# A second cosine table, fewer zero matmuls and a reordered opening in a fused Fourier filter and max-out kernel

## The chip, the cores and the metric

The kernel runs as one program on one core of a Trainium2 chip. The core has a matrix engine (TensorE, "PE" in the profile; its weight loads are listed apart as "PEld"), VectorE ("DVE"), ScalarE ("ACT"), GpSimd ("POOL") and SyncE ("SP"). Each engine works through its own instructions in the order in which the program gives them, and waits where an operand or a buffer is not ready. TensorE writes into PSUM; VectorE and ScalarE copy from there into SBUF. The metric is the device time of the program in microseconds (us). Several executions were timed, and one of them was recorded by the hardware profiler.

## The reference: what is computed

The input x has 8 batches of 3072 tokens with 256 features. Each batch is filtered along its token axis in the frequency domain, and the result goes through a max-out layer of width 1024:

```python
X = np.fft.rfft(x, axis=1)
F = (filt_r + 1j * filt_i)[None, :, :]
y = np.fft.irfft(X * F, n=x.shape[1], axis=1)     # 8 x 3072 x 256

h1 = y @ w1                                       # 24576 x 1024
h2 = y @ w2
out = np.maximum(h1, h2) @ w_out                  # 24576 x 256, float32
```

## The kernel before, in words

The Fourier transform of length 3072 is split as 128 times 24. The kernel uses max(h1, h2) = h2 + max(h1 - h2, 0): the weights `Wd` hold w1 - w2, the ReLU of `y @ Wd` is multiplied by `Wo`, and the part of h2 is one product with `M` = w2 @ w_out, which is made once. Matrix products are in bf16.

**Stages of one batch.** S1 multiplies the tokens with a table of cosines and sines of length 128 (`C1`, 128x128). S2 multiplies with the twiddle table `U`, in 8 groups of frequencies. VectorE (or GpSimd) multiplies the result with the filter table `F` (the "products", tiles `pq`). S3 goes back with the tables `VP` and `VQ`. S4 multiplies with `G1`, the transpose of `C1`, and gives `yt`. After it come `moe_h` (product with `Wd`, ReLU) and `moe_o` (products with `Wo` and `M`, then the output DMA).

**Two forms.** Batches 1 to 7 take the form of the long steady part: `f1` is S1, its result is transposed by way of DRAM (`ad`, `bt`), and `gen_f2` is S2, products and S3. They are interleaved with `moe_h` and `moe_o` of the batch ahead: a loop of 49 x 8 steps calls `moe_h` and `moe_o`, and a dictionary `todo` says at which step a piece of the next batch's work is issued. Batch 0 has nothing to hide behind, so it takes a form of its own, the opening, in which TensorE transposes and nothing goes through DRAM:

- `first_s1(c)`, c = 0 to 5 (lines 428 to 436): S1 for one loaded chunk of x. Eight matmuls of 128x128x128 whose moving operand is `C1` read as `"p (t b a) -> p b a t"`, that is with a step of four elements; then ScalarE copies 128x1024 into `At`.
- `expand_f(g, ri, E)` (lines 113 to 126): sixteen small matmuls with a selection matrix that bring two rows of the real (ri = 0) or imaginary (ri = 1) filter into the order of `F`; engine `E` copies 128x1024.
- `tables_u`, `sines_u` (lines 205 to 273): some forty VectorE instructions and then ScalarE sines make `U`. `tables_pe` (line 280) transposes `U` into `VP`; `tables_q` (line 294) makes `VQ`.
- `first_t1(g, E)` (lines 438 to 447): eight transposes of `At`, copied into `bt[0]` by `E`.
- `first_s2(g, pool)` (lines 455 to 472): S2 of group g, and the two products. With `pool`, ScalarE first copies half of the PSUM tile to `xs` and GpSimd makes the second product.
- `first_s3(g, pq)` (lines 474 to 488): S3 of group g, 32 matmuls, copied by ScalarE into `Zt`.
- `prep_w(k, E)` (lines 323 to 338): k = 0 and 1 transpose w2 into `w2T`; k = 2 and 3 multiply `w2T` by `Wo` into the two halves of one PSUM tile, and k = 3 copies it to `M`.
- `first_t2(j, E)` (line 490): transposes of `Zt` into `zr[0]`, which `s4` reads.
- `spin(pd, n)` (lines 307 to 309): n matmuls of 128x128x512 whose operands are zeros. Their results are overwritten. There are 14 at the start, one at the head of every `expand_f` and every `first_s1`, and two at the head of every `first_s3`.

**What sets the order.** The program text gives each engine its order; nothing reorders it. PSUM has two buffers under each of two tags, `pa` and `pb` (`bank2`, line 88). Up to the group loop the calls take `pa` and `pb` in turn; in the group loop (lines 601 to 621) `first_s2` takes `pb` and all others take `pa`. A call waits until the last but one user of its tag has been copied out. The group loop goes over n = 0 to 7 with group g = order[n], order = (1, 2, 3, 0, 4, 5, 6, 7), and `first_s3` runs two groups behind `first_s2`. The opening ends where `s4(0)` and the first `moe_h` begin (lines 626 to 637).

The loads are issued by GpSimd: the real filter, six chunks of x of batch 0, the imaginary filter, w1 and w2, the chunks of batch 1, and later `Wo`.

## Time and profile before

| | us |
|---|---|
| median of 8 runs (lowest 546.56, highest 549.3) | 546.82 |
| the profiled execution | 546.95 |
| its span in the trace | 545.0 |
| outside the span in that execution (546.95 - 545.0) | 1.95 |
| TensorE busy | 520.3 (95%) |
| ScalarE busy | 337.3 (62%) |
| VectorE busy | 322.8 (59%) |
| GpSimd busy | 72.7 (13%) |
| first matmul on the filter (after it has landed) | 8.62 |
| first matmul of `s4(0)` | 56.48 |

The times of a timeline are in us from the start of the span. A line gives the start, the length, the engine, the source line, the operation with output<-input and shapes, the count, and in brackets how long the engine sat idle before it and what ended that. A matmul's length includes its way through the array, so the next one starts before it ends. A busy share in a table by stretches is in us of the stretch.

### The profile page before, as it was taken

The numbers are of one execution on the slowest core, as the hardware profiler recorded it, in microseconds if no ns is written. First come the engines' busy times: TensorE is split into PE (matmuls) and PEld (weight loads), VectorE is DVE, ScalarE is ACT, GpSimd is POOL, SyncE is SP. The second block draws the span as 40 slices with busy tenths as digits, with TensorE's granted clock in tenths as the row PEclk, the third lists the DMA queues.
The fourth block names the chain that finished last, engine by engine and source line by source line (L and its number), as shares of the span: only waits on it lengthen the run. The fifth ranks groups of instructions, "written<-read, shape, count | busy, mean of one in ns | idle before, by whom it ended". The sixth has DMA issues, their size and how long they took to land.

```text
span 545.0 us, 12576 instructions
## 1 busy us (share of the span) xinstructions
PE 520.3 (95%) x5389; PEld 352.0 (65%) x5389; DVE 322.8 (59%) x427; ACT 337.3 (62%) x590; POOL 72.7 (13%) x126
## 2 busy tenths in 40 slices
PE   7988899999999999999999899999999999999992
PEld 3655566667666666676667666666667666677771
DVE  8576759524872476438763677448863788344331
ACT  6866647775787578845775467755775565554540
POOL 6184011011001110021001100021000000000000
PEclk9999999999999999999999999999999999999997
DMA  8972297779477965599378955599377925611111
GB/s 161 285 117 41 112 169 156 174 232 242 110 214 222 213 164 161 161 215 218 110 218 201 201 146 163 163 229 212 108 211 191 168 81 144 163 40 78 79 40 77
DMA packets 67596, 87.07 MB, mean 160 GB/s; under 512 B 3986, under 2 KB 48276, under 8 KB 66452
## 3 DMA queue, kind: packets, MB, share of 16 engines
q1 hardware_dynamic: 51908, 44.31, 35.9%
q0 software_dynamic: 15632, 41.95, 29.3%
q8 instruction: 42, 0.69, 0.6%
q14 instruction: 14, 0.11, 0.1%
HBM read 53.74 MB, written 47.19 MB: 185 GB/s over the span
## 4 chain that ended last, share of the span: by engine, by line
issue 66%; POOL 6%; PE 4%; POOLq 0%
POOL out_dram L552 4%; POOL xb L101 2%; PE po L546 1%; PE ph L521 1%; PE po L541 0%; PE px L408 0%; PE py L505 0%; POOLq L730 0%; POOLq L552 0%; PE pz L389 0%; POOLq L101 0%
## 5 line engine op out<-in xcount | busy, mean ns | idle before, releaser
L526 ACT ACTIVATE gt<-ph 128x512 bf16<-128x512 f32 x307 | 181.9, 599 | 111.3 <-PE ph L521 110.3
L546 PE MATMUL po<-Wo,gt 128*128 128x256 bf16 x1536 | 229.8, 273 | 0.0
L546 PEld LDWEIGHTS <-gt 128*128 128x128 bf16 x1536 | 150.3, 98 | 57.5
L413 DVE TENSOR_TENSOR pq<-px,F 120x1024 bf16<-120x1024 f32 x112 | 131.7, 1218 | 25.3 <-PE px L408 24.4
L548 DVE COPY ot<-po 128x512 f32<-128x512 f32 x96 | 66.3, 690 | 109.4 <-PE po L546 108.8
L393 ACT ACTIVATE zt<-pz 112x512 bf16<-112x512 f32 x112 | 60.8, 594 | 45.4 <-PE pz L389 40.4
L521 PEld LDWEIGHTS <-Wd 128*128 128x128 bf16 x768 | 69.9, 98 | 25.4 <-issue 11.3
L552 POOL DMA_DIRECT2D out_dram<-ot x48 | 25.8, 538 | 445.1 <-DVE ot L548 415.4
L524 DVE TENSOR_SCALAR gt<-ph 128x512 bf16<-128x512 f32 x77 | 52.9, 687 | 35.2 <-PE ph L521 31.3
L453 ACT ACTIVATE at<-pa 128x512 bf16<-128x512 f32 x77 | 46.2, 601 | 11.5 <-PE pa L354 9.2
L354 PE MATMUL pa<-xb,C 128*128 128x512 bf16 x84 | 31.5, 381 | 0.8 <-DVE zr L451 0.8
L505 PE MATMUL py<-G,zr 128*128 128x128 bf16 x384 | 29.7, 219 | 0.7 <-DVE pq L413 0.7
L389 PE MATMUL pz<-pq,VP 56*64 56x256 bf16 x448 | 28.8, 271 | 1.6 <-DVE pq L413 1.6
L505 PEld LDWEIGHTS <-zr 128*128 128x128 bf16 x384 | 24.9, 98 | 6.0 <-issue 3.4
L389 PE MATMUL pz<-pq,VQ 56*64 56x256 bf16 x448 | 28.1, 268 | 0.0
L101 POOL DMA_DIRECT2D xb<-in_x_dram x48 | 26.0, 547 | 7.6 <-PE pa L433 4.1
L408 PE MATMUL px<-bt,U 48*64 48x256 bf16 x448 | 23.9, 281 | 1.8 <-DMA bt<-ad 1.8
L469 DVE TENSOR_TENSOR pq<-px,F 120x1024 bf16<-120x1024 f32 x13 | 15.3, 1219 | 4.5 <-ACT xs L464 2.0
L408 PEld LDWEIGHTS <-U 48*64 48x64 bf16 x448 | 8.5, 104 | 14.1 <-issue 11.8
L389 PEld LDWEIGHTS <-VP 56*64 56x64 bf16 x448 | 13.4, 106 | 3.7 <-DVE pq L413 2.2
L453 ACT ACTIVATE F<-pf 128x1024 bf16<-128x1024 f32 x12 | 12.1, 1022 | 5.6 <-PE pf L125 5.5
L389 PEld LDWEIGHTS <-VQ 56*64 56x64 bf16 x448 | 13.4, 107 | 0.0
(360 smaller groups left out, 588.3 us busy)
## 6 DMA issues: line engine op xcount, KB each, us to landing
out_dram<-ot POOLq DMA_DIRECT2D x48, 512.0 KB, 4.3
xb<-in_x_dram POOLq DMA_DIRECT2D x48, 256.0 KB, 7.6
ad<-at SPq DMA_DIRECT2D x42, 256.0 KB
bt<-ad SPq DMA_DIRECT2D x28, 384.0 KB
zd<-zt SPq DMA_DIRECT2D x56, 192.0 KB
zr<-zd SPq DMA_DIRECT2D x14, 768.0 KB
wf<-in_moe_w_dram POOLq DMA_DIRECT2D x2, 1024.0 KB, 15.1
Fs<-in_filt_r_dram POOLq DMA_DIRECT2D x1, 768.0 KB, 6.9
```

The source lines that it names most:

```text
L101: G.dma_start(out=t_, in_=src[:, 4 * c:4 * c + 4, :])
L389: TE.matmul(pz[c][64 * k:64 * k + 64, i], W[64 * c:64 * c + 56, 2 * g + i, k], pq[k][64 * c:64 * c + 56, ri, i], start=(ri == 0), stop=(ri ...
L393: S.activation(zt[0:ROWS, c, o:o + 2], pz[c][0:ROWS], AF.Copy)
L413: V.tensor_tensor(pq[k][0:FROWS], px[k][0:FROWS].rearrange("p (o i) d -> p o i d", o=1).to_broadcast([FROWS, 2, 2, D]), F[0:FROWS, :, k, 2 ...
L453: S.activation(out_, in_, AF.Copy)
L505: TE.matmul(py[:, n], zr[b][:, 4 * i + n, 128 * dc:128 * dc + 128], G1, start=True, stop=True)
L521: TE.matmul(ph, Wd[:, dc, 128 * j:128 * j + 128], y_[:, dc].rearrange("p a b -> p (a b)"), start=(dc == 0), stop=(dc == 1))
L524: V.tensor_scalar(gt[tt][:, j], ph, 0.0, None, OP.max)
L526: S.activation(gt[tt][:, j], ph, AF.Relu)
L546: TE.matmul(p_, g_[:, jj, 128 * n:128 * n + 128], Wo[:, jj], start=False, stop=(jj == 7))
L548: V.tensor_copy(ot[tt][:, n - 1:n + 1], po[tt])
L552: G.dma_start(out=dst[:, 4 * i:4 * i + 4], in_=ot[tt])
```

## The change: what it does

- A second cosine table `Ct` is made by one VectorE copy at the end of `table_c`; it holds the values of `C1` in the order in which `first_s1` reads them, so that the moving operand is read without a step.
- `expand_f` and `first_s1` lose their one zero matmul each, and `first_s3` keeps one of two. The zero operand shrinks from 128x512 to 128x128; the zero matmuls read it four times over and still have 512 columns.
- Before the group loop `first_t1(3)` comes ahead of `expand_f(1, 1)` and `first_t1(0)` ahead of `expand_f(2, 1)`. In the loop `first_t1(order[n + 4])` moves from the end of an iteration to its head, ahead of `first_s2` and the products.
- `expand_f(7, 0)` moves from n = 1 to n = 3.
- `prep_w(0)` and `prep_w(1)` move from n = 6 and 7 to n = 4 and 5, ahead of `table_g` in n = 4. `prep_w(2)` and `prep_w(3)` move from behind the loop into n = 6, and the copy to `M` goes from VectorE to ScalarE.
- One piece of S1 of batch 1 more (`f1(1, 1)`) is done before `first_t2(0)`, and the rest move up by one.

```diff
     def expand_f(g, ri, E):
         pf = bank2([128, 2, 2, D], FP32, "pf")
-        spin(pf[:, 0].rearrange("p u d -> p (u d)"), 1)
...
-    Sp = init.tile([128, 512], BF16)
+    Sp = init.tile([128, 128], BF16)
...
+    Ct = init.tile([128, 128], BF16)
+
     def table_c():
...
+        V.tensor_copy(Ct.rearrange("p (b a t) -> p t b a", b=2, a=2), C1.rearrange("p (t b a) -> p t b a", b=2, a=2))
...
     def spin(pd, n):
         for _ in range(n):
-            TE.matmul(pd, Sp[:, 0:128], Sp, start=True, stop=True)
+            TE.matmul(pd, Sp, Sp.rearrange("p (o x) -> p o x", o=1).to_broadcast([128, 4, 128]), start=True, stop=True)
...
     def first_s1(c):
         pa = bank2([128, 2, 2, 2, 4, T], FP32, "pa")
-        spin(pa[:, 0].rearrange("p b a n t -> p (b a n t)"), 1)
         for dh in range(2):
             for n in range(4):
                 TE.matmul(pa[:, dh, :, :, n], xb[0, c][:, n, 128 * dh:128 * dh + 128],
-                          C1.rearrange("p (t b a) -> p b a t", b=2, a=2), start=True, stop=True)
+                          Ct.rearrange("p (b a t) -> p b a t", b=2, a=2), start=True, stop=True)
...
     def first_s3(g, pq):
         pz = bank2([128, 2, 512], FP32, "pz")
-        spin(pz[:, 0], 2)
+        spin(pz[:, 0], 1)
...
     first_t1(2, V)
     tables_q(1, S)
+    first_t1(3, V)
     expand_f(1, 1, S)
-    first_t1(3, V)
+    first_t1(0, V)
     expand_f(2, 1, S)
-    first_t1(0, V)
     pend = []
     ring = ["pa"]
     for n, g in enumerate(order):
+        if n < 4:
+            first_t1(order[n + 4], V)
         pend.append(first_s2(g, n in (0, 2, 4)))
-        if n == 1:
-            expand_f(6, 0, S)
+        if n in (1, 3):
+            expand_f(6 + n // 2, 0, S)
         if n < 6:
             expand_f(order[n + 2], 1, S)
         if n == 0:
             load_wo()
         if n == 1:
             fix_f()
-            expand_f(7, 0, S)
         if n in (1, 3, 5):
             prep_wd(n // 2, *wf)
-        if n < 4:
-            first_t1(order[n + 4], V)
+        if n > 1:
+            first_s3(*pend.pop(0))
+        if n in (4, 5):
+            prep_w(n - 4, S)
         if n == 4:
             table_g()
-        if n > 1:
-            first_s3(*pend.pop(0))
-        if n > 5:
-            prep_w(n - 6, S)
+        if n == 6:
+            prep_w(2, S)
+            prep_w(3, S)
     first_s3(*pend.pop(0))
-    prep_w(2, V)
     first_s3(*pend.pop(0))
-    prep_w(3, V)
     zr[0] = zrpool.tile([128, N2, D], BF16, tag="zr", name="zr")
     f1(1, 0, V)
+    f1(1, 1, V)
     first_t2(0, V)
...
-    f1(1, 1, S)
+    f1(1, 2, S)
     s4(0)
-    f1(1, 2, V)
+    f1(1, 3, V)
...
-    for c in range(3, 12):
-        plan(int(0.6 * (c - 2)), f1, 1, c, (S, V)[c % 2])
+    for c in range(4, 12):
+        plan(int(0.6 * (c - 3)), f1, 1, c, (S, V)[c % 2])
```

## The prediction, made before the result was known

> **What bounds the kernel now.** I read the page first, then busy time by stretches, then the timelines of the opening engine by engine, then the waits of the steady part. By stretches (PE, PEld, DVE, ACT, POOL busy us, granted clock, DMA share, GB/s):

> ```profile
> 8.60:22.40 13.80, 13.10 (x221) 8.81 (x220) 9.94 (x17) 10.37 (x13) 4.66 (x8) 1.00 1.09 256
> 22.40:26.80 4.40, 4.39 (x68) 3.12 (x68) 1.98 (x3) 3.30 (x4) 0.00 (x0) 1.00 1.07 309
> 26.80:52.40 25.60, 22.80 (x499) 12.98 (x497) 18.40 (x18) 17.83 (x22) 17.42 (x13) 1.00 0.55 87
> 52.40:56.50 4.10, 2.84 (x52) 2.11 (x52) 1.98 (x3) 0.81 (x1) 0.00 (x0) 1.00 0.00 0
> ...
> 100.00:515.00 415.00, 410.94 (x3943) 281.09 (x3941) 243.25 (x295) 265.11 (x482) 38.65 (x73) 1.00 0.68 169
> ```

> The steady part is TensorE's, at 99%, so a start that is earlier by some time should end the program earlier by as much. The change lies in the four stretches above it. The first two are TensorE's as well, but part of that is zero matmuls. One round of the S1 stretch in TensorE's timeline:

> ```profile
> 12.06 0.39 PE L309 MATMUL pa<-Sp 128*128 128x512 bf16 x1
> 12.29 1.09 PE L433 MATMUL pa<-C,xb 128*128 128x128 bf16 x8
> 13.20 0.40 PE L309 MATMUL pf<-Sp 128*128 128x512 bf16 x1
> ```

> The starts give the spacing: zero matmul 0.23, S1 0.91, zero matmul 0.33, expansion (line 125, 13.53) 0.55, round 2.02 with the next zero matmul at 14.08. So 0.56 of each 2.02 us is zeros. In the group loop (iteration n = 4) it is a chain through ScalarE:

> ```profile
> 39.87 0.41 PE L460 MATMUL px<-bt,U 48*64 48x256 bf16 x8
> 40.21 0.39 PE L309 MATMUL pf<-Sp 128*128 128x512 bf16 x1
> 40.53 0.62 PE L125 MATMUL pf<-Fs,Sel 96*32 96x256 bf16 x16
> ...
> 42.28 0.59 PE L309 MATMUL pz<-Sp 128*128 128x512 bf16 x2 [0.96 <-ACT F L453]
> ...
> 43.30 0.41 PE L460 MATMUL px<-bt,U 48*64 48x256 bf16 x8
> ```

> The reader is to see that S3's bank is the one that ScalarE is emptying: S2 0.34, zeros 0.32, expansion until it lands 0.62, copy 1.02 (line 453, from 41.20) with 0.1 of handing over, two zeros 0.53, S3 0.50, together 3.43, and the iteration took 43.30 - 39.87 = 3.43. All three zero matmuls lie on that chain.

> **The method.** I write down each engine's order after the change and go through it with spacings from the rows: S2 0.34, expansion 0.55, transposes of `At` 0.55 (8 of them), S3 0.50, a zero matmul 0.32, `w2T` transposes 0.56, a half of M 0.78; ScalarE copies 1.02 (0.81 for `Zt`, 0.60 for `xs`), VectorE 1.22 for a filter, 1.15 to 1.22 for a product, 0.69 for `bt`, `at`, `zr`; 0.05 from an end to the one who waits. Done with the order of before, this comes 0.2 to 0.4 us late against the trace: 22.60 for 22.40 at the first transposes of `At`, 27.07 for 26.83 at the first S2, 52.82 for 52.44 at the last S3.

> **First stretch, 8.62 to the first transposes of `At` (22.40).** Eleven zero matmuls go (five at expansions, six at S1), 0.23 to 0.33 each. S1 itself reads `Ct`: its eight matmuls take 0.91 now, and the same shape with an unstepped operand (line 505) starts its successor after 0.44 (56.48 to 56.92). The price lies between 0.44 and 0.91 (its output pattern, which stays, may be what is slow); I take 0.50, nearest to the row of the same shape. TensorE's round would be about 1.1, so TensorE stops being the limit. Next is VectorE, through the copy that makes `Ct`:

> ```profile
> 2.53 0.29 DVE L198 TENSOR_TENSOR uc<-uc,rc 128x128 f32<-128x128 f32 x1
> 2.74 0.15 DVE L211 TENSOR_SCALAR col<-pid 128x1 f32<-128x1 f32 x1
> ...
> 2.86 1.00 ACT L202 ACTIVATE C<-uc,zero 128x32 bf16<-128x32 f32 x4 [0.84 <-DVE uc L198]
> ```

> The copy stands between the first two lines and has to wait for the sines to end at 3.86. Its own length is between 0.11 (memset of 128x64) and 0.96 (line 287, twelve times as large); I take 0.25, by the 0.23 of a 128x128 pass (line 197). The some forty instructions of `tables_u` queue behind it: they start at 4.15 instead of 2.74, 1.4 late, so VectorE's first filter copy starts at 14.3 instead of 12.97 (the first line-451 row there), and the sines of `U` wait until 13.8. From there: filter copies end 15.5, 16.7, 17.9, 19.2. The fifth expansion needs the bank that the first of these frees: 15.55 (TensorE then has idled 1.8 us). S1 of chunk 3 at 16.1, expansion 16.8, S1 of chunk 4 at 17.3; `VP`'s transposes wait for the last sines, 18.5; S1 of chunk 5 at 19.1 (its x landed at 6.25 + 10.9 = 17.15, so no DMA ends this); `At` 19.8 to 20.8; the transposes at 20.9 instead of 22.40. **Gain 1.5.** Without the 1.4 on VectorE it would be 1.1 more; were the copy 0.96 long, 0.7 less.

> [...] Line 433 spaces its matmuls 0.114, line 505 0.055. [...]

> **Second stretch, to the first S2 (26.83).** Before: four transposes, one `VQ` product, two expansions, two zeros: 2.20 + 0.53 + 1.10 + 0.64 = 4.47, measured 4.43. After: the zeros go, `first_t1(4)` moves in: 2.75 + 0.53 + 1.10 = 4.38. **Gain 0.05.** The `bt` copies on VectorE (0.69 in each 0.55 to 1.1) keep pace.

> **Third stretch, S2 of n = 0 to the last S3 (25.61).** Iteration lengths before, from the starts of line 460 (26.83, 28.69, 32.81, 36.42, 39.87, 43.30, 45.56, 47.50) and the last S3 (52.44): 1.9, 4.1, 3.6, 3.4, 3.4, 2.3, 1.9, 4.9. After, by the walk: 1.5, 2.9, 2.9, 3.0, 3.3, 3.3, 2.8, 2.9, in sum 22.65. n = 1 loses one of three expansions (to n = 3) and three zeros. In n = 2 S3 now waits for VectorE, which copies the hoisted `bt` behind two products (to 31.15). In n = 3 it waits for the copy of filter 7, which came in. n = 4 to 6 take `w2T` and M in, each piece waiting for the 1.02 of a filter copy or of the `w2T` copy ahead; the M copy on ScalarE (0.60) frees the bank for S3 of group 6. In the tail S3 of group 7 waits for the last products: S2 45.0, products 45.5 and 46.65 to 47.87, S3 at 47.9. GpSimd is no limit: `w2b` is ready at 34.0 (used at 38.0), `Wd` at 42.9; `Wo` lands by 37 (used at 43.5); SP has nothing in this part. **Gain 2.95.**

> **Fourth stretch, last S3 to `s4(0)` (4.04).** Before, M's copy stood between:

> ```profile
> 54.03 0.69 DVE L451 CAST M<-pm 128x512 bf16<-128x512 f32 x1 [3.33 <-PE pm L335]
> ...
> 54.78 0.71 PE L494 MATMUL pt<-I,Zt 128*128 128x128 bf16 x8 [0.48 <-DVE M L451]
> ...
> 55.52 0.69 DVE L451 COPY zr<-pt 128x1024 bf16<-128x1024 bf16 x1 [0.20 <-PE pt L494]
> ```

> After: S3 lands 0.65, `Zt` 0.81, the added `f1` 0.27, transposes 0.77, `zr` 0.74, `f1(1, 2)` 0.21, in sum 3.45 to 3.5. **Gain 0.55.** The added `f1`'s VectorE copy (0.69) fits while TensorE transposes.

> **Steady part.** One `f1` fewer in it (0.22 a matmul of 512): **gain 0.2.** `f1_read` stays at step 5 with `f1` done a step earlier, and TensorE's waits for a transfer after 57 us are small: line 408 for `bt`, 1.8 us in two waits.

> **Sum.** 1.5 + 0.05 + 2.95 + 0.55 + 0.2 = 5.25; against its own lateness the walk is worth up to 0.4 more. I take 5.5: 546.95 - 5.5 = 541.4 for the profiled execution, which lies 0.13 above the median. Own range of this case 540.0 to 542.8 (`Ct`'s copy, S1 between 0.44 and 0.91, the lateness).

> **Rivals.**

> *TensorE's clock falls (slower).* The first 14 zero matmuls start 0.43 apart until 5.46 and then about half that: TensorE begins at half rate and reaches the full one only after 4.2 us of steady work. Without the zeros it is thinly fed: by the walk 0.5 us of matmuls in the 3.05 before 15.55, then 55 to 75% of most stretches. If the rate falls, each us of the opening at half rate costs about 0.33 by the walk (blocks 1.9 times as long, partly within waits). From 17 us of it on (5.5 / 0.33) there is no gain; half rate throughout the group loop (24 us) gives 549, from 12.3 us on 554. Against it: TensorE stood still from 6.8 to 8.62, and the next expansions were spaced 0.55 as later; from 53.95 to 57.88 it had 1.4 us of work in 3.9, and the next `moe_h` pair took 0.59 as always. The granted clock of 1.00 from 0 to 5 us doesn't show that half rate, so it settles nothing. [...]

> *Half of it: some falls.* Three to ten us at half rate: 1 to 3.3 lost, 542.4 to 544.7.

> [...]

> *The opening is shorter and the end isn't.* Transfers would have to set the pace of the steady part; then 545 to 546.9. Against: DMA share 0.68 there and 1.8 us of waits.

> **How the numbers follow.** The forecast 0.58; clock falls for part 0.16; VectorE 0.08; end not earlier 0.05 (0.03 of it within 0.2% of 546.8, which is what the measurement can tell from none); clock low for 17 us or more 0.13. Faster 0.84, same 0.03, slower 0.13. The range leaves out the slow clock (0.13) and a little below: 539.8 to 546.0.

> **What would show it.** Right: lines 309 of the S1 rounds gone; a VectorE wait for `C` of about 1 us before `Ct`, its first filter copy near 14.3; `At` transposes near 20.9, first S2 near 25.3, last S3 near 47.9, `s4(0)` near 51. Wrong: expansions spaced 1.0 instead of 0.55 anywhere after 8.62, S1 of eight near 0.9, or `s4(0)` near 51 with a span above 541.

## The result and the profile after

The changed kernel takes 543.17 us in the median of its 11 runs (540.34 to 545.37), the kernel before 547.38 in 32 runs (546.27 to 550.82). The ratio is 0.9908, with a 95% interval of 0.9889 to 0.9927: about 0.9% faster. The profiled execution took 541.22 us with a span of 539.1, against 546.95 and 545.0.

The forecast was 541.4 for the profiled execution, in a range of 539.8 to 546.0. Direction and range hold, and the profiled execution is 0.2 below the forecast. The median of the runs is 1.8 above it: between the medians the gain is 4.2 us where 5.5 was forecast. The runs spread over 5 us, and where the median of the kernel before lies 1.1 above its fastest run, that of the changed kernel lies 2.8 above. This is the part that needed explaining.

First the stretches of the prediction in the changed kernel, cut at the same events (columns as before: length, busy us of PE, PEld, DVE, ACT, POOL, granted clock, DMA share, GB/s):

```profile
8.60:20.84 12.24, 9.46 (x210) 6.54 (x210) 10.99 (x20) 9.98 (x12) 4.13 (x7) 0.86 1.09 231
20.84:25.31 4.47, 4.47 (x75) 3.64 (x74) 2.67 (x4) 3.60 (x4) 0.53 (x1) 1.00 1.03 384
25.31:47.79 22.48, 19.10 (x487) 12.78 (x485) 17.75 (x17) 18.14 (x23) 17.35 (x13) 1.00 0.69 115
47.79:51.24 3.45, 1.99 (x40) 1.36 (x41) 1.98 (x3) 0.85 (x2) 0.00 (x0) 1.00 0.00 0
```

The four lengths were 13.8, 4.4, 25.6 and 4.0 before. TensorE's busy time in the first stretch fell from 13.10 to 9.46, and its granted clock from 1.00 to 0.86. The timeline shows the second table's copy on VectorE, and what came late for it (start, length, engine, line, operation):

```profile
2.45 0.29 DVE L199 TENSOR_TENSOR uc<-uc,rc 128x128 f32<-128x128 f32 x1
2.78 1.00 ACT L203 ACTIVATE C<-uc,zero 128x32 bf16<-128x32 f32 x4 [0.76 <-DVE uc L199]
...
3.81 0.56 DVE L206 COPY Ct<-C 128x128 bf16<-128x128 bf16 x1 [1.06 <-ACT C L203]
...
4.04 0.33 DVE L214 TENSOR_SCALAR col<-pid 128x1 f32<-128x1 f32 x1
...
14.33 4.61 DVE L453 CAST F<-pf 128x1024 bf16<-128x1024 f32 x4
```

VectorE waits 1.06 us for `C1`. The row of the copy is 0.56 long, but the next one starts 0.23 after it, against 0.25 in the prediction. VectorE's first filter copy starts at 14.33 where it was 12.97. TensorE's rounds in the same stretch:

```profile
8.86 1.65 PE L124 MATMUL pf<-Fs,Sel 96*32 96x256 bf16 x32 [2.32 <-DMA Fs<-in_filt_r_dram]
10.44 1.03 PE L435 MATMUL pa<-Ct,xb 128*128 128x128 bf16 x8
11.41 1.04 PE L124 MATMUL pf<-Fs,Sel 96*32 96x256 bf16 x16
12.38 0.70 PE L435 MATMUL pa<-Ct,xb 128*128 128x128 bf16 x8
13.01 0.62 PE L124 MATMUL pf<-Fs,Sel 96*32 96x256 bf16 x16
...
15.60 0.62 PE L124 MATMUL pf<-Fs,Sel 96*32 96x256 bf16 x16 [1.41 <-DVE F L453]
```

The expansion at 11.41 takes 1.04, the one at 13.01 takes 0.62: behind the pause from 6.5 to 8.86 the granted clock went to 0.50, from 9.17 to 12.58, and then back to 1.00. Little or nothing of this can have reached the end: until 15.60 TensorE waited 1.41 us for VectorE's first filter copy to end, which the prediction had at 15.55.

In the group loop TensorE waits where the prediction has it wait, in n = 2 for the hoisted `bt` and in n = 3 for the copy of filter 7:

```profile
31.14 0.38 PE L312 MATMUL pz<-Sp 128*128 128x512 bf16 x1 [0.45 <-DVE bt L453]
...
34.70 0.38 PE L312 MATMUL pz<-Sp 128*128 128x512 bf16 x1 [0.62 <-ACT F L455]
```

The end of the opening (from two views, TensorE's and VectorE's timeline):

```profile
49.27 0.38 PE L357 MATMUL pa<-xb,C 128*128 128x512 bf16 x1 [0.58 <-ACT Zt L490]
49.48 0.71 PE L496 MATMUL pt<-I,Zt 128*128 128x128 bf16 x8
...
50.29 0.68 DVE L453 COPY zr<-pt 128x1024 bf16<-128x1024 bf16 x1
...
51.02 0.38 PE L357 MATMUL pa<-xb,C 128*128 128x512 bf16 x1 [0.83 <-DVE zr L453]
51.24 0.61 PE L507 MATMUL py<-G,zr 128*128 128x128 bf16 x8
```

VectorE's copy of M is gone from this chain, and `s4(0)` starts at 51.24 instead of 56.48.

### The profile page after: what moved, and what is told of

It is laid out like the page before. It is cut to its first block, busy times and chain, and to the rows that moved or that the text cites. A ratio compares the mean times of both kernels' runs of the same rounds, so it can differ in the third digit from the quotient of the medians.

```text
span 539.1 us, 12518 instructions
## 1 busy us (share of the span) xinstructions
PE 511.7 (95%) x5359; PEld 349.1 (65%) x5359; DVE 322.2 (60%) x427; ACT 337.6 (63%) x591; POOL 72.6 (13%) x126
## 4 chain that ended last, share of the span: by engine, by line
issue 48%; PE 24%; POOL 4%; DVE 0%; POOLq 0%
PE ph L523 9%; PE po L548 9%; POOL out_dram L554 3%; PE po L543 2%; PE pz L392 1%; POOL xb L101 1%; PE px L411 1%; PE pa L357 1%; PE py L507 1%; DVE pq L416 0%; POOLq L733 0%; POOLq L554 0%; POOLq L101 0%
## 5 line engine op out<-in xcount | busy, mean ns | idle before, releaser
L523 PEld LDWEIGHTS <-Wd 128*128 128x128 bf16 x768 | 69.9, 98 | 25.3 <-issue 11.1
L124 PE MATMUL pf<-Fs,Sel 96*32 96x256 bf16 x256 | 10.6, 296 | 4.6 <-DMA Fs<-in_filt_r_dram 2.3
```

The source lines that it names most:

```text
L523: TE.matmul(ph, Wd[:, dc, 128 * j:128 * j + 128], y_[:, dc].rearrange("p a b -> p (a b)"), start=(dc == 0), stop=(dc == 1))
```

## Experiments

Two theories were to be told apart at first. Theory Z: the zero matmuls on TensorE's way were the cost, and cutting them is the gain. Theory O: the new order, the second table and the move of w2.wo (w2 @ w_out, made by `prep_w`) made it. Theory C stood beside them: a thinly fed TensorE loses its clock, and that makes the spread.

A measure that the falls of the clock before 25 us don't touch is the length from the first S2 to `s4(0)`, called the loop below: 29.65 us before (26.83 to 56.48), 25.93 after (25.31 to 51.24). Unless it is said otherwise, its granted clock was 1.00 in the profiled execution.

### e1: the zero matmuls cut, nothing else

```diff
 before.py, expand_f and first_s1:
-        spin(..., 1)
 first_s3:
-        spin(pz[:, 0], 2)
+        spin(pz[:, 0], 1)
```

> The kernel before with one edit alone: the zero matmuls of expand_f and first_s1 go and first_s3 keeps one. Theory Z (the zeros on TensorE's way were the cost): the walk through the queues gives s4(0) at 51.3 against 56.5, nearly the whole gain: time 0.990 to 0.992 of before. Theory O (the new order, the second table and w2.wo made the gain): at most the zeros that no wait hid, s4(0) at 54 or later, ratio 0.995 to 1.0. Theory C (TensorE's clock falls when it is thinly fed): the granted clock of the runs lies between 0.984 and 0.991 instead of 0.994 and the runs with the lower clock are 1 to 2 us longer each 0.003.

Measured: ratio 0.991 (0.9879 to 0.9942), so the whole gain of the change within the intervals. The loop takes 26.17, 3.48 of the 3.72 that the change takes off. `s4(0)` came at 52.75 and not at 51.3, because the clock fell twice, from 10.94 to 14.35 and from 21.18 to 24.59. The second fall lies in the dense stretch between the first transposes and the first S2, which took 5.43 where it takes 4.4. The stretches of e1:

```profile
7.50:10.94 3.44, 2.16 (x44) 1.66 (x47) 3.23 (x11) 1.73 (x2) 1.44 (x2) 1.00 1.12 216
10.94:14.35 3.41, 3.41 (x45) 2.20 (x46) 3.31 (x7) 2.55 (x4) 1.09 (x2) 0.50 1.13 207
14.35:21.18 6.83, 6.01 (x128) 4.13 (x126) 4.43 (x4) 5.79 (x9) 1.59 (x4) 1.00 1.05 258
21.18:24.59 3.41, 3.41 (x34) 2.29 (x34) 1.38 (x2) 1.46 (x2) 0.53 (x1) 0.50 1.04 405
```

The granted clock (the last column but two) goes straight to 0.50 and back, in pieces of 3.41 us. Over the runs, clocks of 0.990 to 0.991 go with 541.1 to 542.1 us, clocks of 0.980 to 0.986 with 543.2 to 544.5. Theory Z holds, and C in so far as the clocks came out near what it said (0.980 to 0.991); O falls as the main cause.

### e2: the zero matmuls put back into the changed kernel

```diff
 after.py, expand_f and first_s1:
+        spin(..., 1)
 first_s3:
-        spin(pz[:, 0], 1)
+        spin(pz[:, 0], 2)
```

> The changed kernel with all zero matmuls of before put back (30 more), everything else as changed. Theory Z: s4(0) at about 54.2 by the walk, so about half of the gain or less is left: ratio to before 0.994 to 0.997. Theory O: s4(0) stays near 51.5, ratio 0.990 to 0.992. Theory C: the granted clock is back at 0.994 in every run and the runs lie within 1 us of each other, apart from those outliers that before has too.

Measured: ratio 0.9965 (0.9941 to 0.9988); `s4(0)` at 54.39, the loop 27.91. Theory Z's numbers hold. So the order is worth 1.74 in the loop while the zeros stand (29.65 to 27.91), but only 0.24 once they are gone (26.17 to 25.93): the two gains are not additive. Theory C's expectation failed: with all zeros in place the clock of the runs still went from 0.985 to 0.995, and the slowest took 549.2. So the zeros of before, where they stood, don't keep the clock in every run.

### e3: more zeros at the very start

```diff
-    spin(bank2([128, 2, 512], FP32, "pd")[:, 0], 14)
+    spin(bank2([128, 2, 512], FP32, "pd")[:, 0], 23)
```

> The changed kernel with 23 instead of 14 zero matmuls at the very start, so that TensorE is busy until about 8.3 us, when the filter lands. Theory C: the half-rate stretch that the changed kernel's trace shows from 8.86 to 12.4 is gone (expansions spaced 0.55, granted clock 0.993 or more in most runs); s4(0) moves by less than 0.3 us in a run without other falls, since that stretch waits for x and VectorE anyway, but the spread of the runs shrinks if that fall is the one that varies. Rival: the falls that make the spread come later in the opening; then the clock goes up by 0.003 in all runs and the spread stays at 4 to 5 us.

Measured: ratio 0.9918 (0.9886 to 0.995), no better. The fall at 9 us was gone, but a longer one came:

```profile
7.18:10.59 3.41, 1.84 (x42) 1.31 (x40) 3.23 (x13) 1.35 (x2) 1.07 (x3) 1.00 1.02 194
10.59:14.00 3.41, 3.20 (x45) 1.78 (x43) 3.27 (x6) 2.47 (x4) 1.58 (x3) 0.50 1.12 207
14.00:17.40 3.40, 2.73 (x32) 2.03 (x31) 3.32 (x6) 2.72 (x4) 1.06 (x2) 0.50 1.16 229
17.40:20.80 3.40, 3.40 (x94) 2.49 (x93) 1.95 (x3) 2.63 (x4) 0.53 (x1) 0.50 0.96 267
20.80:24.24 3.44, 3.33 (x25) 2.27 (x24) 1.26 (x2) 2.05 (x2) 0.53 (x1) 0.50 1.04 414
```

The clock fell at 10.59, after 3.4 us in which TensorE was busy for 1.84, and stayed down for 13.65 us, four times 3.41, although TensorE was busy nearly all of it. `s4(0)` came at 53.65, 2.4 later than in the changed kernel with its one fall. Theory C as put forward is too simple: with the first pause filled, a longer fall came behind shorter ones. The median of the runs is no lower than the changed kernel's, although three of the six have a clock of 0.990 to 0.992.

### e4: the copy of Ct later on VectorE

```diff
 table_c, last line:
-        V.tensor_copy(Ct..., C1...)
 tables_u, after V.tensor_scalar(na, pa_, -1.0, None, OP.mult):
+        V.tensor_copy(Ct..., C1...)
```

> The changed kernel with the copy that makes Ct moved on VectorE behind the first thirteen instructions of tables_u, by when ScalarE has finished C1; nothing else. Theory of the prediction (VectorE's wait for C1 is the first stretch's limit): VectorE's first filter copy starts at about 13.3 instead of 14.3, the transposes of At at 19.9 instead of 20.8, s4(0) 0.9 to 1.0 earlier, ratio to before 0.2% lower than the changed kernel's. Rival (the arrival of x and the sines take over): s4(0) moves by less than 0.4.

Measured: VectorE's first filter copy at 12.93, 1.4 earlier (1.0 was expected). The transposes of `At` came at 20.84 all the same, and `s4(0)` at 51.42; ratio 0.9918 (0.9888 to 0.9948). The clock was at 0.50 from 9.6 to 16.4 in this execution, and from 9.97 to 15.90 TensorE's S1 and expansions were spaced 0.96 to 1.08, where it is 0.56 from 16.70 to 17.26, so a fall can have hidden the gain. A second fall to 0.50, from 50.6 to 54.0, came in TensorE's waits just ahead of `s4(0)`. Whether x would have hidden the gain too was left for e8 and e9.

### e5: the second table alone

```diff
 before.py:
-    Sp = init.tile([128, 512], BF16)
+    Sp = init.tile([128, 128], BF16)
+    Ct = init.tile([128, 128], BF16)
+        V.tensor_copy(Ct..., C1...)          # end of table_c
-                          C1.rearrange("p (t b a) -> p b a t", b=2, a=2), ...
+                          Ct.rearrange("p (b a t) -> p b a t", b=2, a=2), ...
```

> The kernel before with the second table alone: Ct copied in table_c and read by first_s1, and the zero operand of 128x128 that makes room for it; all zero matmuls and the whole order as before. Walk theory: S1 of eight goes from 0.91 to about 0.5, VectorE's first filter copy to 14.3; TensorE is still the limit of the first stretch, the transposes of At come at 21.6 instead of 22.4, s4(0) at 55.5 to 55.9 instead of 56.5: 1 us. [...]

Measured: S1 of eight takes 0.56 (15.02 to 15.58) or 0.44 (16.67 to 17.11) to the zero matmul behind it at full rate where `C1` takes 0.91. This time only the table that is read, and so the operand's step, differs. `s4(0)` came at 55.93, 0.55 earlier, with one fall to 0.50 from 10.2 to 13.6. The loop was 29.65, as before, and the ratio 0.9994 (0.9974 to 1.0014): no measurable gain.

### e6: w2.wo inside the loop alone

```diff
 before.py, group loop:
+        if n in (4, 5):
+            prep_w(n - 4, S)
         if n == 4:
             table_g()
-        if n > 5:
-            prep_w(n - 6, S)
+        if n == 6:
+            prep_w(2, S)
+            prep_w(3, S)
...
+    f1(1, 1, V)                               # ahead of first_t2(0)
```

> The kernel before with the third item of the change alone: prep_w moved into n = 4, 5 and 6, M copied by ScalarE, one f1 more ahead of first_t2(0). Walk theory: with the zeros in place s4(0) comes 0.7 earlier (55.8), all of it between the last S3 and s4(0), where VectorE's copy of M stood; the steady part is one f1 shorter, 0.2; ratio 0.998. Rival (it only shifts work from the tail into iterations 4 to 6): the last S3 comes as much later as the tail gets shorter, s4(0) within 0.3 of 56.5.

Measured: ratio 1.0005 (0.9986 to 1.0023); the loop 29.42, 0.23 shorter. The rival was right: from the last S3 to `s4(0)` it is 0.6 shorter, and the last S3 is 0.4 later.

### e7: w2.wo and filter 7 put back in the changed kernel

```diff
 after.py, group loop: prep_w, table_g, the copy of M, f1 and expand_f(7, 0) as in before.py
```

> The changed kernel with prep_w, the copy of M, the order of f1 and expand_f(7, 0) put back where they were; the second table, the hoisted transposes and the cut zeros stay. Walk theory: without the zeros moving w2.wo and filter 7 costs more in n = 3 to 6 than it gives in the tail; putting them back brings the last S3 to about 46.4 (48.0 in the changed kernel) and s4(0) to 50.4 (51.24), the steady part gets one f1 (0.2) back: ratio to before 0.1% below the changed kernel's at an equal clock. Rival (w2.wo inside the loop is a gain with or without zeros): s4(0) at 51.7 to 52. Each 3.4 us of half rate in the opening adds 0.6 to 1.2 to either.

Measured: the loop 24.49, 1.44 shorter than in the changed kernel (0.8 was expected), with one `f1` (about 0.2) more left for the steady part. So without the zeros the two moves together are a loss of about 1.2. By the starts of S2, the iterations n = 3 to 6 take 1.72, 2.63, 1.93 and 1.86 in e7 where the changed kernel takes 2.90, 3.23, 3.15 and 3.02. n = 1, which has filter 7 back, takes 3.81 for 2.88, and from the S2 of n = 7 to `s4(0)` it is 8.33 for 6.33. No run has one of the two moves without the other. `s4(0)` came at 51.58 nevertheless, since the clock was down from 14.27 to 21.1 (0.53 and 0.50 in the two halves). TensorE's timeline of e7:

```profile
12.77 0.62 PE L435 MATMUL pa<-Ct,xb 128*128 128x128 bf16 x8
15.60 1.05 PE L124 MATMUL pf<-Fs,Sel 96*32 96x256 bf16 x16 [2.20 <-DVE F L453]
16.57 1.03 PE L435 MATMUL pa<-Ct,xb 128*128 128x128 bf16 x8
17.54 1.04 PE L124 MATMUL pf<-Fs,Sel 96*32 96x256 bf16 x16
```

Here VectorE's late filter copy makes the 2.2 us pause, and the fall begins in it; the stretch of 3.41 us before it had TensorE busy for 2.20. The ratio was 0.9908 (0.9876 to 0.994), with runs from 540.4 (clock 0.991) to 545.6 (0.984).

The profiled execution of e7 also lost its clock in the steady part: TensorE waited 1.8 us for `bt` just after 360 us, and from 365 to 370 the granted clock was 0.66, that is half rate for 3.4 of the 5 us. From `s4(0)` to the end it took 491.8 us, against 487.9 in the changed kernel. The executions of e3 and e2 have a fall between 350 and 400 us too (490.0 us each to the end), after waits of 1.77 and 1.61 for `bt`. The wait alone doesn't decide: e7 waited 1.86 for `bt` at 301 us as well and kept its clock (1.00 from 300 to 350, with TensorE idle for 2.20 of it), as the changed kernel did after 1.35 and e8 after 1.54, both near 361 (1.00 from 350 to 400, with TensorE idle for 1.68 and 1.96).

### e8: that, and the copy of Ct later

```diff
 e7, with the move of e4
```

> The kernel of e7 with the copy that makes Ct behind thirteen instructions of tables_u as well: the version that the walk puts first. Walk theory: s4(0) at 49.5 if TensorE keeps its full rate through the first stretch, ratio to before 0.987 to 0.989; with half rate from 10 to 15 us, as in e4, VectorE's earlier start is hidden again and s4(0) is that of e7 (50.4). Rival (the falls of the clock eat what the order saves): ratio no lower than 0.991, with a granted clock below 0.988.

Measured: ratio 0.99 (0.9862 to 0.9938); six runs from 538.51 (clock 0.994) to 545.81 (0.981). The loop is 24.47, and `s4(0)` came at 50.31 with two falls, at 8.8 and near 19 (0.51 in 8.8 to 12.2 and in 19.0 to 22.4). Both theories fit at once: the run with the clock of 0.994 is the fastest so far, and the lower the clock of the others, the longer they took.

### e9: zeros only where TensorE waits anyway

```diff
 e8:
-    spin(bank2([128, 2, 512], FP32, "pd")[:, 0], 14)
+    spin(bank2([128, 2, 512], FP32, "pd")[:, 0], 23)
 first_s1, before its matmuls (they wait for x):
+        spin(pa[:, 0].rearrange("p b a n t -> p (b a n t)"), 1)
```

> The kernel of e8 with zero matmuls only where TensorE waits anyway: 23 instead of 14 at the start, and one at the head of each first_s1, which waits for x. Theory (idle TensorE makes the clock fall): fewer stretches of half rate in the first 20 us, granted clock 0.99 or more in most runs, median time 1 to 2 us below that of e8 with the same fastest run. Rival (the falls don't follow from the idle share; e3 fell at 10.6 after a stretch with TensorE busy three quarters of the time): granted clocks spread from 0.98 to 0.995 as in e8, median not lower.

Measured: ratio 0.9852 (0.9832 to 0.9871), the lowest so far; its interval lies below that of the changed kernel, and overlaps that of e8. One run of e8 (538.51) is faster than all four. The four runs took 539.26 to 540.06 with clocks of 0.993 to 0.995. The profiled one, with 0.995, has no fall before TensorE's last work: its clock reads 1.00 in every stretch up to 530 us, and only the tail from there on (0.80), in which TensorE is busy for 0.00, takes the mean below 1. Stretches of 3.4 us of the profiled execution:

```profile
5.10:8.50 3.40, 3.40 (x14) 1.34 (x13) 3.30 (x16) 1.48 (x3) 2.34 (x7) 1.00 0.98 204
8.50:11.90 3.40, 3.07 (x63) 1.95 (x63) 3.23 (x8) 2.72 (x3) 1.44 (x2) 1.00 1.13 218
11.90:15.30 3.40, 3.02 (x56) 1.99 (x54) 3.30 (x8) 3.06 (x5) 1.60 (x3) 1.00 1.15 216
15.30:18.70 3.40, 2.81 (x103) 2.04 (x101) 2.67 (x3) 3.07 (x5) 1.08 (x3) 1.00 1.07 220
```

TensorE is busy for 2.81 or more in each, and the clock stays at 1.00. The transposes of `At` come at 20.09 and `s4(0)` at 49.09, with the loop at 24.50. That answers what e4 left open: with VectorE's filter copies at 12.94 and no fall, x doesn't hide the gain, or not all of it: the transposes come 0.75 before the changed kernel's. The theory holds where the pauses of the first 20 us are filled, and not where one is (e3).

### e10: the same with ones instead of zeros

```diff
-    V.memset(Sp, 0.0)
+    V.memset(Sp, 1.0)
```

> The kernel of e9 whose filler operands are ones instead of zeros (their results are overwritten all the same). [...] Rival (data don't matter): same spread of clocks as e9 and the warm-up ending 4 to 4.5 us after the first matmul.

Measured: ratio 0.9849 (0.983 to 0.9869), clocks 0.992 to 0.994, `s4(0)` at 48.93. No difference from e9 can be told: zeros or ones as the filler's data made none here. With e9, eight timed runs have clocks of 0.992 to 0.995 and lie between 539.1 and 540.1, where one of the six runs of e8 has such a clock.

### e11: the last zero of S3 cut as well

```diff
 e8, first_s3:
-        spin(pz[:, 0], 1)
```

> The kernel of e8 without the last zero matmul of first_s3. Walk theory: s4(0) 0.5 earlier at the same clock. Theory of the falling clock: more half rate in the group loop, which is then fed at 45 to 60%; each 3.4 us of it costs 0.6 to 1.2, so the median is not lower than e8's and falls appear between 25 and 45 us.

Measured: ratio 0.9907 (0.9889 to 0.9925), clocks 0.978 to 0.985 in all six runs. The group loop of the profiled execution:

```profile
34.00:38.00 4.00, 2.66 (x97) 1.91 (x91) 3.48 (x4) 3.77 (x6) 4.00 (x3) 1.00 0.35 50
38.00:49.00 11.00, 10.65 (x221) 7.64 (x210) 6.56 (x7) 6.91 (x8) 5.26 (x4) 0.53 0.32 51
```

The loop took 26.71, 2.2 longer than with that zero matmul, as it ran at half rate from 38.0 to 48.3. This is the clearest case for theory C: with eight matmuls taken out of TensorE's way the loop got longer, and five of its six runs have clocks of 0.978 to 0.981, where e8 has 0.981 to 0.994. The whole times can't be told apart from e8's.

### e12: no second table

```diff
 e7 without Ct: first_s1 reads C1, no copy in table_c
```

> The kernel of e7 without the second table: first_s1 reads C1 again and VectorE does not wait for it; zeros cut, transposes hoisted. Walk theory (with the zeros gone the table's gain on TensorE and its 1.36 us on VectorE cancel): transposes of At and s4(0) within 0.2 of e7's at an equal clock. Rival (the table is a gain of its own): s4(0) 0.8 to 1.0 later than without half rate in e7 (50.4).

Measured: ratio 0.9895 (0.987 to 0.992); the loop 24.48, as in e7. The first transposes came at 21.73 with the clock down until 15.1 (0.50 from 8.5 to 15). No gain of the table can be seen once the zeros are gone; since the falls of e7 and e12 lie in different places, a difference of some tenths in the first stretch stays open.

## Why the prediction was right, and where it was not

**The sum.** Its terms, predicted and measured in the profiled execution: first stretch 1.5 and 1.57; second 0.05 and -0.05; third 2.95 and 3.12 (the last S3 starts at 47.8); fourth 0.55 and 0.60; steady part 0.2 and 0.66; outside the span 0 and -0.17. Together 5.25 (5.5 taken) and 5.73. The method of following each engine's queue with the rows of before gave the first transposes at 20.9 (20.84 measured), the first S2 at 25.3 (25.31), the last S3 at 47.9 (47.79) and `s4(0)` at 51.4 (51.24). The iterations of the group loop, 1.5, 2.9, 2.9, 3.0, 3.3, 3.3, 2.8 and 2.9 by the prediction, took 1.54, 2.88, 2.88, 2.90, 3.23, 3.15, 3.02 and 2.88 (the last to the last S3). So the mechanism holds, term by term, up to `s4(0)`. That the whole comes within 0.2 of 541.4 is in part luck: in the profiled execution of the changed kernel no fall cost much, and the 0.66 of the steady part is within what that part varies by. From `s4(0)` to the end, the executions without a fall there took 487.5 to 489.1 us.

**The wait that replaces the old limit.** That the copy of `Ct` would hold VectorE for 1.4 us and make it the limit of the first stretch is what the trace shows: 1.36 late, and TensorE waits for it at 15.60. What it costs was given as 1.1; e9 and e10, with the copy out of the way and no fall, have the transposes 0.75 and 0.93 earlier, with a zero matmul in each S1. S1 with `Ct`, taken as 0.50, has a spacing of 0.58 to the expansion behind it (16.15 to 16.73). The 0.44 of the row of the same shape was not reached there; ahead of a zero matmul it was, with the same output pattern (e5, 16.67 to 17.11). The 0.08 for VectorE as the bound found no support: the copy of `Ct` has a spacing of 0.23, not 0.96, and S1 0.58, not 0.91.

**What the parts are worth.** The prediction did not say what each part of the change gives by itself. The runs do. Cutting the zeros alone gives 3.48 of the 3.72 us of the loop (e1); on top of all the rest it gives 1.98 (27.91 to 25.93, e2). All the rest gives 1.74 while the zeros stand and 0.24 without them. The table alone gives no measurable time (e5) and w2.wo inside the loop alone none (e6). The hoisted transposes, with S3 ahead of `table_g`, are worth some 1.7 in the loop without zeros (26.17 to 24.48 from e1 to e12), most of which the moves of w2.wo and filter 7 take away again. The prediction had added up the iterations right, but had not asked what the loop would be without these two moves. The loss of 0.8 that e7's expectation names was worked out only after the result was known; 1.44 was measured.

**The step that was misjudged: the clock.** The forecast put 0.58 on an undisturbed clock and 0.16 on "some falls", with 542.4 to 544.7 for it. The runs fell in that rival's place: the median is 543.17, and eight of the twelve executions have a clock of 0.988 or less. Those with 0.989 or 0.990 took 540.3 to 541.2, those with 0.984 or 0.985 took 543.3 to 545.4. The profiled one had a single fall in the opening, where TensorE waited for VectorE afterwards. One of the prediction's own signs of being wrong did appear in it: expansions spaced 0.97 instead of 0.55, at 11.41. The argument against the rival was that before's TensorE stood still from 6.8 to 8.62 and was thinly fed from 53.95 to 57.88 without losing its rate. Both were single observations from one execution, and falls don't come each time: by their mean clocks runs of the kernel before have them too. Its runs beside these experiments went from 0.987 (550.3 and 551.9 us) to 0.995 (546.1 to 547.6). The price, 0.33 per us of half rate, is of the right size in the opening: e3, with some 10 us more of it than the changed kernel, came 2.4 later at `s4(0)`, 0.24 per us. In the steady part, where TensorE is busy 99% of the time, an estimate is half the length of the fall, 1.7 us, besides the wait ahead of it: e3 took 2.1 more to the end than the changed kernel, of which 0.4 is its longer wait for `bt` (1.77 for 1.35).

The clock is not the whole of the spread. In the changed kernel the runs at 0.989 and 0.990 and those at 0.984 and 0.985 lie 3 us apart. A mean lower by 0.005 over 540 us is 5.4 us more of half rate, which by itself can cost 2.7 at most, a little less than that. Waits for a transfer that come with a fall are a candidate for the rest, which these runs don't settle. In e12 three runs with one clock, 0.987, took 540.0, 541.3 and 543.1.

**What brings a fall on.** The half-rate stretches of the openings last 3.41 (changed kernel), 6.8 (e4), 10.2 (e11) and 13.65 us (e3). The one of the changed kernel follows 3.4 us with TensorE busy for 1.09, but the clock also fell after 3.4 us with TensorE busy for 1.84 (e3) or 2.16 (e1), in e3 with no pause above 1.1 us. The fourteen falls that begin in the openings of these traces all follow a stretch of 3.41 us with TensorE busy for 2.59 (e1, ahead of 21.18) or less. But such a stretch doesn't always bring a fall: the clock stayed at 1.00 after one with 2.00 (changed kernel, 12.6 to 16.0), 1.96 (e3, 51.55 to 54.96), 1.82 (e7, 7.45 to 10.86) and 1.57 (before, 5.46 to 8.87). So thin feeding goes ahead of every fall here, and what else it takes is open.

## What to carry to other kernels

Filler matmuls were neither waste nor harmless here. On the chain that sets the end they cost 3.48 of the 29.65 us of the loop (e1). In the waits of the first 20 us they cost nothing that can be seen, and the clock kept its rate (e9, e10). Cut them from the chain and try them where TensorE waits for data in any case. In one and the same order of the work that took the ratio from 0.99 to 0.9852 (e8, e9; the two intervals overlap from 0.9862 to 0.9871, so the median is not shown to be lower). The runs lay within 0.8 us in place of 7.3. When several reorderings come in one change, test each with and without the others: gains on one chain overlap, and one that pays while another cost stands can become a loss when it is gone.
